# A fused attention and MLP kernel: pair sums for the middle heads of the second batch, and three block pairs begun before the attention ends

## The chip, the cores and the metric

The kernel runs on one core of a Trainium2 chip. The metric is the device time of one execution in microseconds (us), smaller is better. TensorE does the matmuls, VectorE and ScalarE the elementwise work, GpSimd a part of it, and SyncE (SP) issues most transfers.

## The reference

Eight batches, twelve heads, 448 positions, head size 64; then an MLP over the 3584 tokens.

```python
q_n, k_n = rmsnorm(q, g_q), rmsnorm(k, g_k)        # over the head's 64 numbers
scores = matmul(q_n, k_n.T) / sqrt(64)
attn = exp(scores - max); attn /= attn.sum(-1)
x = matmul(attn, v)                                # [3584, 768]: tokens x (heads * 64)
h = x @ w_in                                       # d_ff = 2048
out = gelu_tanh(h) @ w_out
```

All inputs and the output are float32; the kernel's matmuls take bf16.

## The kernel before

**Tiling.** One attention is one batch: three groups of four heads (c = 0, 1, 2; the "middle heads" are c = 1), seven tiles of 64 positions each. A *unit* (c, t) is the scores of one tile for four heads (`unit`, L335: four matmuls of 64x448 into one PSUM tile of two banks) and its exp (`exp`, L343, on ScalarE). So a batch has 21 units, 0 to 20; units 7 to 13 are the middle heads'. From the second attention on TensorE works in quarters of 64x64, four matmuls side by side.

**Behind the units.** "s" is the sum over the exps, a product with ones; "x" is the product with V (both `products`, L387). For some groups VectorE adds exps before "s" so that fewer matmuls are needed: `added(b, c)` says how many tiles are merged into one, and `add_exps` has the steps A (tiles 0,1 plus 2,3: two pair sums, L355), B (plus 4,5, L358), F (the two into one, L360), G (plus tile 6, L362). In batch 1 the first group adds seven tiles, the last six, and the middle group none: its "s" reads the seven exps, 28 matmuls. After "s" VectorE transposes the sums (T, `turned`, L397), takes reciprocals (R, `recip`, L402), spreads them (S, `spread`, L409) and multiplies "x" with them (M, `quad_x`, L422) into `xT`, which the MLP reads.

**Batch pipeline.** The attention of batch b+1 runs on TensorE mixed with the second MLP layer of the batch before (`quartered`, L495). After it comes the first layer of the batch (`mm1_turn`, L537), two 128-column blocks of w_in ("a pair") in one PSUM tile, in two turns, with a gelu per pair (L543). The last heads' `xT` comes late, so a pair can begin with the chunks of the first eight heads (`early`, four of six chunks) and take the last two (`late`) afterwards. `attention` begins pairs 0 and 1 that way at its end.

**What sets the order.** Every engine's order is written out by hand. `SECOND` (L577) is the second attention's: its first string mixes second-layer steps ("3r" is three steps of four matmuls) with units, "s" and "x"; its second string is the order of VectorE, where small letters and K, L are hooks for other work (`extra`): L0 and L1 load batch 2's q and k, K0 applies the gain to the DMA-transposed k of batch 1's last heads (`gain`, L325) and lets GpSimd go on to the squares for batch 2 (`gpsimd_waits`, L795, then L164), a0 to a5 reduce these squares (L173). VectorE's queue is in order: an entry that waits holds all behind it.

**PSUM.** Four tiles are handed out in turn by `pair`; the second layer holds one while it accumulates, so units, "s" and "x" take turns in three. `rsqrt_last` also takes one as scratch space.

**Transfers.** SP issues q and k loads, the stores and the DMA transposes (`dma_trans`, L319), in program order. `late_loads` and `late_transposed` first write one element of the destination on VectorE, so that SP issues the transfer only when VectorE has come to that place in its queue. GpSimd issues w_in, w_out and v on a queue of its own; the last part of w_out is wanted in the second attention.

**First attention.** `first_attention` (batch 0) runs the units with lists of side work per slot (`side`, `mid`); slot n of `mid` comes behind unit n and its exp.

Of the kernel before, what the change touches and what calls it, by code (L numbers as in the profile page):

```python
# [17 lines left out]
def kernel(  # L18
# [11 lines left out]
    nc = tc.nc  # L30
# [9 lines left out]
    NT = S // R  # L40
    NCH = H // 4
    HP = H // 2
# [95 lines left out]
    def late_loads(b, c):  # L138

        for n in "qk":  # L140
            for go in load(b, c, n):
                nc.vector.memset(raws[n, b, c][:1, 0, 0, :1], 0.0)
                go()
# [167 lines left out]
    def trans(b, c, eng=nc.vector):  # L311
        for n in "qk":
            turn(b, c, n)
            put(b, c, n, eng=eng)
# [12 lines left out]
    exs, ess, oas, scs = {}, {}, {}, {}  # L327
# [18 lines left out]

    def added(b, c):

        return NT - 1 if b > 1 else (NT - 1, 0, NT - 2)[c] if b else 0

    def add_exps(b, c, step):
        ex = exs[b, c]
# [18 lines left out]
    def products(b, c, what, lo=0, hi=NT):  # L371

        if lo == 0 and steady():
            o = oas["o", c, what] = pair("o")
            oas[what] = oas[c, what] = [o[:, r, :S] for r in range(2)]
        elif lo == 0:
            oas[what] = spare.pop() if spare else [o[:, :S] for o in oall]
        o = oas[what]
        es = [exs[b, c][:, t] for t in range(NT)]
        if not what and added(b, c):  # L380
            es[:added(b, c) + 1] = [ess[b, c][:, 0]]
        n = len(es)
        for i in range(lo, min(hi, n)):
            for r in range(2):
                rs = slice(r * R, (r + 1) * R)
                for a in range(2):
                    nc.tensor.matmul(  # L387
                        o[r][a * D:(a + 1) * D],
                        vb[b % 2][rs, 2 * c + a, i] if what else ones[rs], es[i][rs, a],
                        start=(i == 0), stop=(i == n - 1),  # L390
                    )
# [156 lines left out]
    def mm1_pair(i, cs=range(HP), b=0, js=range(2)):  # L548
# [19 lines left out]
    early, late = range(HP - 2), range(HP - 2, HP)  # L568
# [8 lines left out]
    SECOND = (  # L577
        "3r u 5r uu 8r u 8r uu 8r u 5r u 4r u 7r us 4r u 4r u 3r uu 4r x 1r usu 3r u 6r u 2r u 5r"
        " uu 10r x 6r sx",
        "A0 L0 B0 F0 G0 L1 T0 R0 K0 S0 a0 M0 a1 T1 a2 R1 a3 S1 A2 a4 B2 a5 F2 M1 T2 R2 S2 M2",  # L580
        {6: 0, 14: 1, 21: 2},
    )

    def attention(b, side, extra, ends):

        order, dve, evictions = STEADY if b > 1 else SECOND
        at = 0 if b % 2 else 3
        if b > 1:
            m, lo = HD // 2, b % 2 * HD
            tiles = [[(i, 0, HD), (i, HD, d_model)] for i in range(at, at + 3)]  # L590
            tiles.append([(6, lo, lo + m), (6, lo + m, lo + HD)])
        else:
            tiles = [[(0, 0, HD), (1, 0, HD)], [(2, 0, HD), (0, HD, d_model)],
                     [(1, HD, d_model), (2, HD, d_model)]]
        full, made = {}, {("unit", -1)}

        def second_layer():
            for k, parts in enumerate(tiles):
                def finished(o, k=k):
                    full[k] = o  # L600
                    made.add(("full", k))
                yield from quartered(parts, finished, late=b == 1 and k == 0)

        m2 = second_layer()
        units = [(c, t) for c in range(NCH) for t in range(NT)]
        scalar = []
        for n in range(len(units) + 1):
            if n in evictions:
                scalar.append(("E", evictions[n]))
            if n < len(units):  # L610
                scalar.append(("u", n))
        vector = [(w[0], int(w[1:] or 0)) for w in dve.split()]

        def needs(w, c):
            n = c * NT
            return {
                "u": [("unit", c)] + [("x", 0), ("T", 0)] * (c >= 2 * NT), "E": [("full", c)],
                "A": [("u", n + t) for t in range(4)], "B": [("u", n + 4), ("u", n + 5)],
                "G": [("u", n + 6)], "T": [("s", c)], "M": [("x", c)] + [("p", 1)] * (c == NCH - 1),
            }.get(w, [])  # L620

        def run(w, c, eng):
            if w == "u":
                exp(b, *units[c])
            elif w == "E":
                evict(b - 1 - (c == 3 and b % 2), tiles[c], full[c], eng)
            elif w in "ABFG":
                add_exps(b, c, w)
            elif w == "T":
                turned(c)  # L630
            elif w == "R":
                recip()
            elif w == "S":
                spread()
            elif w == "M":
                quad_x(b, c)
            else:
                for fn in extra.get(w + str(c), ()):
                    fn()
            made.add((w, c))  # L640

        def go_on():
            for queue, eng in ((vector, nc.vector), (scalar, nc.scalar), (vector, nc.vector)):
                while queue and made.issuperset(needs(*queue[0])):
                    run(*queue.pop(0), eng)

        n = {"u": 0, "s": 0, "x": 0}
        for fn in extra.get("first", ()):
            fn()
        for word in order.split():  # L650
            if word.endswith("r"):
                for _ in range(int(word[:-1])):
                    next(m2)
                    go_on()
                continue
            for w in word:
                k = n[w]
                n[w] += 1
                if w == "u":
                    for fn in side.get(k, ()):  # L660
                        fn()
                    unit(b, *units[k])
                    made.add(("unit", k))
                else:
                    last = added(b, k)
                    assert {("u", t) for t in range(k * NT, (k + 1) * NT)} <= made
                    assert w == "x" or not last or ("FG"[last - NT + 2], k) in made
                    products(b, k, "sx".index(w))
                    made.add((w, k))
                go_on()  # L670
        assert next(m2, None) is None and not scalar and vector == [("M", NCH - 1)]
        for fn in ends:
            fn()
        nc.scalar.preload_act_table_set(GELU_SET)
        if b == 1:
            for m in "qk":
                square(2, NCH - 1, m, nc.scalar)
        mm1_turn(b, 0, 0, early, begin=True)
        mm1_turn(b, 1, 0, early, begin=True)
        mm1_turn(b, 0, 1, early)  # L680
        mm1_turn(b, 1, 1, early)
        made.add(("p", 1))
        go_on()

# [172 lines left out]
    def turn_new(c, ts):  # L857
# [37 lines left out]
           (17, lambda: products(0, 1, 1, 3), lambda: quad_x(0, 1),  # L895
            lambda: total(1, 0, "q")),
           (18, lambda: spared(), lambda: products(0, 2, 0, 0, 3)),
           (20, lambda: products(0, 2, 0, 3, 5), lambda: products(0, 2, 1, 0, 5),
            lambda: products(0, 2, 0, 5, 6))]
    first_attention(plan(*side), plan(*mid))  # L900

# [4 lines left out]
    def late_transposed(b, c):  # L906

        for n in "qk":
            dst = kT if n == "k" else qT_of(b)
            nc.vector.memset(dst[:1, c, 0, 0, :1], 0.0)  # L910
        transposed(b, c)
# [8 lines left out]
    for b in range(B):  # L920
        m1, side, extra, ends = [], [], [], []
        if b == 0:
# [5 lines left out]
                  (2, lambda: total(1, 1, "q"), lambda: total(1, 1, "k"),  # L928
                   lambda: normed(1, 0, "q", nc.vector), lambda: rsqrt_last(1),
                   lambda: normed_both(1, 1, nc.vector)),  # L930
                  (6, lambda: trans(1, 0, nc.scalar), lambda: late_transposed(1, 2)),
                  (7, lambda: trans(1, 1))]
            extra += [("L0", lambda: late_loads(2, 0)), ("L1", lambda: late_loads(2, 1)),
                      ("a1", lambda: late_loads(2, 2)),
                      ("K0", lambda: gain(1, 2))]

            for n in "qk":
# [38 lines left out]
        for f in range(nf // 2 if b == 0 else nf):  # L976
            i, part = f // 4 * 2, f % 4
            if b == 0:
                if f == 2:
                    mm1(0, 5)  # L980
                    square(1, 1, "k", nc.scalar)
                elif f > 2:
                    mm1_pair(f)
            elif f == 1:
                mm1_turn(b, 0, 1, late)
                mm1_turn(b, 1, 1, late)
                mm1_turn(b, 0, 0, late, end=True)
            elif f == 3:
                mm1_turn(b, 1, 0, late, end=True)
            elif part == 1:  # L990
                mm1_turn(b, i, 0, range(HP), begin=True)
                mm1_turn(b, i + 1, 0, range(HP), begin=True)
                mm1_turn(b, i, 1, range(HP), end=True)
            elif part == 3:
                mm1_turn(b, i + 1, 1, range(HP), end=True)
            for fn in m1.get(f, ()):
                fn()
# [47 lines left out]
```

## Time and profile before

| what | us |
|---|---|
| median of 3 runs | 390.71 |
| the runs | 393.07, 390.71, 390.48 |
| the profiled execution's own time | 391.54 |
| its span, first to last instruction | 389.6 |
| TensorE busy | 380.9 |
| ScalarE busy | 278.7 |
| VectorE busy | 236.1 |
| GpSimd busy | 125.3 |

The span is one profiled execution; its own time is some 2 us more than the span, as launch and end lie outside. A row of a timeline has the start in us from the span's start, the length, the engine, the line and operation, what it writes and reads, and in brackets the idle time of the engine before it and what ended it. In the chain of work that ended last, a matmul's piece runs from the end of the piece before to its own end. "Time to landing" of a transfer is from its issue to the last byte's semaphore.

### The profile page before, as it was taken

How to read it: one execution, taken by the hardware profiler on the slowest of the kernel's cores; microseconds unless marked ns; L12 is line 12 of the kernel's file. 1: busy time of each engine (PE TensorE's matmuls, PEld its weight loads, DVE VectorE, ACT ScalarE, POOL GpSimd, SP SyncE). 2: the span in 40 equal slices, each digit the busy share in tenths (PEclk: the TensorE clock that was granted, in tenths of full speed). 3: DMA queues.
4: the chain of work that ended last, by engine and by line, in shares of the span. 5: the costliest groups of instructions: out<-in, count | busy, mean ns of one | idle time of the engine just before them, and what ended most of it. 6: DMA issues, size and time to landing. Idle time of an engine off the chain costs nothing.

```text
span 389.6 us, 17545 instructions
## 1 busy us (share of the span) xinstructions
PE 380.9 (98%) x8060; PEld 294.2 (76%) x8060; DVE 236.1 (61%) x367; ACT 278.7 (72%) x353; POOL 125.3 (32%) x108
## 2 busy tenths in 40 slices
PE   7899999999999999999999999999999999999996
PEld 5565577777888788877888788877888778887664
DVE  5998837975697259835589256953598204980010
ACT  6995499767994689757996589946897449944300
POOL 5986505384005540083102740064400900000000
PEclk9999999999999999999999999999999999999999
DMA  8999997999714992369822995159622721120033
GB/s 258 326 231 210 210 163 247 266 229 236 152 44 94 248 208 60 84 133 234 171 69 64 203 235 106 44 102 268 98 76 54 123 45 42 44 65 4 2 82 81
DMA packets 64446, 54.68 MB, mean 140 GB/s; under 512 B 37620, under 2 KB 60020, under 8 KB 64372
## 3 DMA queue, kind: packets, MB, share of 16 engines
q1 hardware_dynamic: 53936, 41.33, 44.0%
q0 software_dynamic: 10128, 11.80, 18.4%
q8 instruction: 63, 1.03, 1.1%
q10 hardware_dynamic: 308, 0.43, 0.3%
q14 instruction: 11, 0.09, 0.1%
HBM read 45.61 MB, written 11.01 MB: 145 GB/s over the span
## 4 chain that ended last, share of the span: by engine, by line
PE 92%; ACT 4%; DMA 1%; POOL 1%; SPq 0%; issue 0%; DVE 0%; DVEq 0%
PE t L537 33%; PE t L495 32%; PE t L387 9%; PE t L335 7%; PE t L463 5%; PE t L556 4%; ACT ex L343 4%; DMA rawq<-in_q_dram 1%; POOL g L164 1%; PE h L436 1%; PE tp L296 0%; PE o L387 0%; SPq L745 0%; SPq L124 0%; PE os L387 0%
## 5 line engine op out<-in xcount | busy, mean ns | idle before, releaser
L343 ACT ACTIVATE ex<-t,shift 128x896 bf16<-128x896 f32 x168 | 156.2, 1014 | 2.5 <-PE t L335 2.2
L495 PE MATMUL t<-wout,g 64*64 64x384 bf16 (+1 forms) x3456 | 151.2, 305 | 0.7 <-issue 0.7
L495 PEld LDWEIGHTS <-g 64*64 64x64 bf16 x3456 | 113.3, 107 | 20.3 <-issue 1.1
L537 PE MATMUL t<-xT,win 64*64 64x448 bf16 x2688 | 128.6, 349 | 0.0
L537 PEld LDWEIGHTS <-win 64*64 64x64 bf16 x2688 | 96.6, 107 | 30.6
L543 ACT ACTIVATE g<-t 128x896 bf16<-128x896 f32 x56 | 50.5, 915 | 57.2 <-PE t L537 57.2
L173 DVE TENSOR_REDUCE ss<-sq 128x14 f32<-128x896 f32 (+3 forms) x45 | 44.6, 996 | 53.5 <-ACT sq L162 48.9
L335 PE MATMUL t<-qT,kT 64*64 64x448 bf16 x672 | 58.7, 351 | 1.8 <-ACT ex L343 0.8
L355 DVE TENSOR_TENSOR es<-ex 128x1792 bf16<-128x1792 bf16 x20 | 21.2, 1058 | 32.2 <-ACT ex L343 32.2
L278 POOL TENSOR_TENSOR nrmq<-rawq,rinv 128x896 bf16<-128x896 f32 (+1 forms) x21 | 34.8, 1659 | 15.6 <-ACT rinv L205 12.0
L795 POOL COPY mark<-es 1x1 bf16<-1x1 bf16 x6 | 1.1, 176 | 117.2 <-DVE es L362 112.6
L278 POOL TENSOR_TENSOR nrmk<-rawk,rinv 128x896 bf16<-128x896 f32 x20 | 33.6, 1680 | 0.0
L387 PE MATMUL t<-ex,vb 64*64 64x448 bf16 x588 | 32.1, 350 | 0.0
L335 PEld LDWEIGHTS <-kT 64*64 64x64 bf16 x672 | 25.5, 106 | 7.6 <-DVE kT L305 1.6
L397 DVE STREAM_TRANSPOSE st<-t 128x448 f32<-128x448 f32 x42 | 24.7, 626 | 9.1 <-PE t L387 9.1
L387 PEld LDWEIGHTS <-vb 64*64 64x64 bf16 x672 | 23.6, 107 | 7.0 <-issue 0.8
L409 DVE STREAM_TRANSPOSE rb<-rc 128x896 f32<-128x896 f32 (+1 forms) x25 | 26.7, 1067 | 0.3
L422 DVE TENSOR_TENSOR xT<-t,rb 128x896 bf16<-128x896 f32 x21 | 22.8, 1086 | 1.4 <-ACT ex L343 0.7
L701 DVE COPY osb<-t 128x384 f32<-128x384 f32 (+1 forms) x4 | 2.0, 508 | 35.2 <-PE t L463 35.2
L513 ACT COPY osb<-t 128x768 f32<-128x768 f32 (+1 forms) x18 | 12.6, 701 | 14.0 <-PE t L495 14.0
L164 POOL TENSOR_TENSOR sq<-rawq 128x896 f32<-128x896 f32 (+1 forms) x9 | 13.6, 1514 | 27.4 <-DVE ss L173 27.4
L358 DVE TENSOR_TENSOR es<-es,ex 128x1792 bf16<-128x1792 bf16 x20 | 21.3, 1063 | 0.7 <-ACT ex L343 0.7
(103 smaller groups left out, 314.3 us busy)
## 6 DMA issues: line engine op xcount, KB each, us to landing
rawq<-in_q_dram SPq DMA_DIRECT2D x22, 448.0 KB, 4.7
rawk<-in_k_dram SPq DMA_DIRECT2D x22, 448.0 KB, 5.5
out_dram<-osb SPq DMA_DIRECT2D x42, 192.0 KB, 2.7
vb<-in_v_dram POOLq DMA_DIRECT2D x6, 672.0 KB, 6.8
win<-in_moe_w_in_dram POOLq DMA_DIRECT2D x8, 384.0 KB, 12.4
wout<-in_moe_w_out_dram POOLq DMA_DIRECT2D x3, 768.0 KB, 17.9
out_dram<-osb SPq DMA_DIRECT2D x24, 96.0 KB, 4.0
vb<-in_v_dram POOLq DMA_DIRECT2D x2, 448.0 KB, 15.8
```

What stands on the lines that cost most here:

```text
L173: nc.vector.reduce_sum(sss[b][:, seat(b, c), "qk".index(n), hs, ts], squares(b, c, n, hs, ts), axis=AX.X)
L278: eng.tensor_mul(nrms[n, b, c][:, ts].rearrange("p t a d -> p a t d"), raws[n, b, c][:, :, ts], root[:, :, ts].to_broadcast([P, 2, m, D]),)
L335: nc.tensor.matmul(sc[r * R:(r + 1) * R, a, :S], kT[rs, c, t, r], qT[b][rs, c, :, r], start=True, stop=True,)
L343: nc.scalar.activation(exs[b, c][:, t], scs.pop((b, c, t))[:, :, :S], AF.Exp, scale=scale, bias=shift)
L358: nc.vector.tensor_add(es, es, ex[:, 4:6])
L387: nc.tensor.matmul(o[r][a * D:(a + 1) * D], vb[b % 2][rs, 2 * c + a, i] if what else ones[rs], es[i][rs, a], start=(i == 0), stop=(i == n ...
L397: nc.vector.transpose(st[:, r].rearrange("p a b -> p (a b)"), o[r])
L409: nc.vector.transpose(oas["rb"][:, rs].rearrange("p r s -> p (r s)"), rc.to_broadcast([128, (rs.stop - rs.start) * m, 32]),)
L422: nc.vector.tensor_mul(xT[b][:, 2 * c:2 * c + 2], oas["o", c, 1][:, :, :S], oas["rb"])
L495: mm = nc.tensor.matmul(o[a * R:(a + 1) * R, bank, :hi - lo], g[rs, f, at:at + R], wout[rs, f, lo:hi], start=(n == 0), stop=(n == len(step ...
L537: mm = nc.tensor.matmul(h[a * R:(a + 1) * R, j, :S], win[rs, c, at:at + R], xT[b][rs, c], start=begin and c == cs[0], stop=end and c == cs ...
L543: nc.scalar.activation(g[:, 2 * i:2 * i + 2, (b % 2) * S:(b % 2 + 1) * S], h[:, :, :S], AF.Gelu_apprx_tanh,)
```

## The change

1. `added(1, 1)` becomes 3: VectorE does step A for the middle heads of batch 1 (a new entry A1 behind R0 in VectorE's order), and their "s" reads two pair sums and the last three exps, five tiles instead of seven.
2. At the end of batch 1's attention a third pair (2) begins with the first eight heads' chunks, both turns; later, at f = 5, pair 2 gets its last chunks, ends, and pair 3 begins.
3. In the first attention one step of the last heads' sums moves from slot 20 to slot 19.
4. The two DMA transposes for batch 1's last heads move from f = 6 of batch 0's first layer to L0, behind the first A0; the loads of batch 2's first heads move from L0 to the start of the attention. On SP the loads now stand ahead of the transposes, and the first stores and the next loads behind them.

```diff
     def added(b, c):
-        return NT - 1 if b > 1 else (NT - 1, 0, NT - 2)[c] if b else 0
+        return NT - 1 if b > 1 else (NT - 1, 3, NT - 2)[c] if b else 0
...
         if not what and added(b, c):
-            es[:added(b, c) + 1] = [ess[b, c][:, 0]]
+            es[:added(b, c) + 1] = [ess[b, c][:, i] for i in range(1 + (added(b, c) == 3))]
...
-        "A0 L0 B0 F0 G0 L1 T0 R0 K0 S0 a0 M0 a1 T1 a2 R1 a3 S1 A2 a4 B2 a5 F2 M1 T2 R2 S2 M2",
+        "A0 L0 B0 F0 G0 L1 T0 R0 A1 K0 S0 a0 M0 a1 T1 a2 R1 a3 S1 A2 a4 B2 a5 F2 M1 T2 R2 S2 M2",
...
         mm1_turn(b, 0, 1, early)
         mm1_turn(b, 1, 1, early)
+        if b == 1:
+            mm1_turn(b, 2, 0, early, begin=True)
+            mm1_turn(b, 2, 1, early)
...
-           (20, lambda: products(0, 2, 0, 3, 5), lambda: products(0, 2, 1, 0, 5),
+           (19, lambda: products(0, 2, 0, 3, 4)),
+           (20, lambda: products(0, 2, 0, 4, 5), lambda: products(0, 2, 1, 0, 5),
...
-                  (6, lambda: trans(1, 0, nc.scalar), lambda: late_transposed(1, 2)),
+                  (6, lambda: trans(1, 0, nc.scalar)),
...
-            extra += [("L0", lambda: late_loads(2, 0)), ("L1", lambda: late_loads(2, 1)),
-                      ("a1", lambda: late_loads(2, 2)),
+            extra += [("first", lambda: late_loads(2, 0)), ("L0", lambda: late_transposed(1, 2)),
+                      ("L1", lambda: late_loads(2, 1)), ("a1", lambda: late_loads(2, 2)),
...
+            elif b == 1 and f == 5:
+                mm1_turn(b, 2, 1, late)
+                mm1_turn(b, 2, 0, late, end=True)
+                mm1_turn(b, 3, 0, range(HP), begin=True)
```

More of the change, by code (lines that the diff above doesn't have):

```diff
@@ L666, in attention @@
                     assert {("u", t) for t in range(k * NT, (k + 1) * NT)} <= made
-                    assert w == "x" or not last or ("FG"[last - NT + 2], k) in made
+                    assert w == "x" or not last or ({3: "A", 5: "F", 6: "G"}[last], k) in made
                     products(b, k, "sx".index(w))
```

## The prediction

> **What bounds the kernel now.** I read the page first (busy shares, the chain that ended last), then busy time by stage, then the chain piece by piece around the edits, and last VectorE, ScalarE, GpSimd and the DMA queues in order of time from 48 to 80 us, where the edits lie.
>
> ```profile
> span 389.6 us, 17545 instructions
> PE 92%; ACT 4%; DMA 1%; POOL 1%; SPq 0%; issue 0%; DVE 0%; DVEq 0%
> 28.00:50.00 22.00, 22.00 (x170) 12.24 (x160) 18.96 (x46) 12.02 (x15) 12.68 (x11) 1.00 1.14 210
> 50.00:76.80 26.80, 26.10 (x599) 19.66 (x601) 19.32 (x36) 24.03 (x32) 8.31 (x10) 1.00 1.02 221
> 95.00:121.90 26.90, 26.90 (x703) 22.83 (x696) 20.89 (x30) 24.14 (x29) 2.81 (x4) 1.00 0.51 118
> ```
>
> The columns of the stages are length, then busy time of PE, weight loads, VectorE, ScalarE and GpSimd, the granted clock, the DMA share and GB/s. TensorE ends the chain for 92% of the span, at clock 1.00, and from 28 us on it has no idle time to the third attention but for 0.70 us, in the second attention (50.00 to 76.80). So matmul time that is taken away there is worth its full length, and so is every new stall: nothing later gives it back. The third attention on is not edited and moves as a block.
>
> The second attention, piece by piece, in the chain (start, length, what):
>
> ```profile
> 60.75 0.70 issue
> 65.83 0.19 PE t L335 x4
> 66.02 1.32 PE t L387 x28
> 67.35 0.19 PE t L335 x4
> 69.19 0.28 PE t L335 x4
> 76.80 18.22 PE t L537 x384
> ```
>
> After the 0.70 us hole come unit 14 (65.83), the sums of the middle heads (66.02), unit 15 (67.35) and unit 17 (69.19, 0.28 instead of 0.19: it waited a little).
>
> **What the change takes away.** The middle heads' sums go from 28 matmuls to 20: two of the pairs stand for four exps. From the row at 66.02, 8/28 of 1.32 us is **0.38 us**. In the first attention one step of four sum matmuls (1.32/7 = **0.19 us**) goes ahead of the last unit's scores, where TensorE idles 0.52 us:
>
> ```profile
> 27.62 0.38 PE L335 MATMUL t<-qT,kT 64*64 64x448 bf16 x4 [0.52 <-ACT ex L343]
> ```
>
> What follows is back to back until 60.75, so everything up to there comes 0.19 us sooner.
>
> **What it adds on VectorE.** The pair addition A1 stands after the reciprocal R0 and ahead of K0 (gain), S0 (spread), a total, M0 (xT of heads 0-3). In order of time before:
>
> ```profile
> 55.32 1.09 DVE L355 TENSOR_TENSOR es<-ex 128x1792 bf16<-128x1792 bf16 x1 [4.35 <-ACT ex L343]
> 61.45 0.33 DVE L402 RECIPROCAL rc<-st 128x28 f32<-128x28 f32 x1
> 61.69 0.35 DVE L325 TENSOR_SCALAR kT<-kT,gcols 128x896 bf16<-128x896 bf16 x1
> 61.96 1.11 DVE L409 STREAM_TRANSPOSE rb<-rc 128x896 f32<-128x896 f32 x1
> 64.00 1.09 DVE L173 TENSOR_REDUCE ss<-sq 128x14 f32<-128x896 f32 x1 [0.94 <-POOL sq L164]
> 65.78 1.09 DVE L422 TENSOR_TENSOR xT<-t,rb 128x896 bf16<-128x896 f32 x1 [0.69 <-ACT ex L343]
> 66.80 1.07 DVE L173 TENSOR_REDUCE ss<-sq 128x14 f32<-128x896 f32 x1
> 68.39 0.64 DVE L397 STREAM_TRANSPOSE st<-t 128x448 f32<-128x448 f32 x1
> 62.11 0.18 POOL L795 COPY mark<-kT 1x1 bf16<-1x1 bf16 x1 [17.52 <-DVE kT L325]
> L343 ACT ACTIVATE ex<-t,shift 128x896 bf16<-128x896 f32 x168 | 156.2, 1014 | 2.5 <-PE t L335 2.2
> 60.35 1.09 ACT L343 ACTIVATE ex<-t,shift 128x896 bf16<-128x896 f32 x1
> 62.04 1.91 ACT L343 ACTIVATE ex<-t,shift 128x896 bf16<-128x896 f32 x2 [0.60 <-PE t L335]
> 67.11 0.42 PE L335 MATMUL t<-qT,kT 64*64 64x448 bf16 x4
> ```
>
> A1 costs 1.09 us by the first row, but its wait costs more. It needs the exps of units 7 to 10, and unit 10's began at 62.04, after the reciprocal was done (61.78); so VectorE stands still, and with it all that is queued. K0 releases GpSimd's mark, which releases its squares, which the total ahead of M0 waits for: from the start of K0 to that total 2.31 us (61.69 to 64.00), then 1.02 us to the earliest start of M0 (66.80 to the next start at 67.82, the same operation).
>
> Who waits for M0: four PSUM tiles take turns and the second layer holds one, so unit 14, the sums and unit 15 use the other three, and unit 15 writes the tile that M0 reads. Before, M0 ended at 66.87 and unit 15 began at 67.11: 0.24 us to spare.
>
> The earliest end of it: exps follow each other by 0.89 us (1.91 for two, less one of 1.014, the mean of the page's group), so unit 10's exp could begin at 60.35 + 0.89 - 0.19 = 61.05 if the hole at 60.75 is gone. It ends at 62.06; A1 runs from 62.10, K0 from 63.13, the total from 65.44, M0 from 66.46 instead of 65.78: **0.68 us late**. The next chain behind M0 is dense on VectorE (total, the transposes of the sums until 69.03), and unit 17 waits for those transposes; from there on VectorE and TensorE were back to back to 76.8. So 0.68 us is carried to the end, and the 0.38 us of saved matmuls vanish in the wait. If the hole stays, unit 10's exp begins at 62.04 - 0.19 = 61.85 and M0 is **1.48 us late**. The trace names no engine as the hole's cause, so I cannot tell; I take the middle, **1.08**.
>
> **What is moved on the DMA queue.** The two loads of batch 2 leave when VectorE is done with batch 1's transposes (about 51.1) instead of at 56.46, and the two DMA transposes leave behind the first A0 (56.4) instead of at 48.43. The stores and the next loads, behind them on SP, come some 2 to 4 us later.
>
> ```profile
> 48.43 1.32 SPq L319 DMA_TRANSPOSE qT<-nrmq  x1
> 49.85 4.29 SPq L319 DMA_TRANSPOSE kT<-nrmk  x1
> 56.46 0.37 SPq L124 DMA_DIRECT2D rawq<-in_q_dram  x1
> qT<-nrmq SPq DMA_TRANSPOSE x1, 10.3
> kT<-nrmk SPq DMA_TRANSPOSE x1, 2.9
> kT<-nrmk SPq DMA_TRANSPOSE x1, 6.2
> ```
>
> The last three rows are times to landing: under the weights' stream, and of two later transposes. From 56.4 and one issue of 1.3 us, kT lands between 60.6 and 63.9, and K0 wants it at 63.13 to 64: hidden by A1's own wait, or late by at most 0.8. I take 0. GpSimd's second pair of squares would want its loads at about 67.5; issued 2 to 4 us after 60.56 they land at 67.5 to 69.5, and the totals that read them come 1.6 us behind: hidden.
>
> The loads now share the engines with the last part of w_out:
>
> ```profile
> L785 POOL DMA_DIRECT2D wout<-in_moe_w_out_dram x1: 723/723/723, 33.7 to 33.7; - x1
> wout<-in_moe_w_out_dram POOLq DMA_DIRECT2D x1, 384.0 KB, 20.5
> 53.58 1.30 PE t L495 x32
> q0 software_dynamic: 354, 0.39, 115.8%
> q0 software_dynamic: 362, 0.32, 97.7%
> q1 hardware_dynamic: 271, 0.07, 25.6%
> rawq<-in_q_dram SPq DMA_DIRECT2D x1, 448.0 KB, 5.7
> q1 hardware_dynamic: 106, 0.19, 104.3%
> ```
>
> It lands at 33.7 + 20.5 = 54.2. TensorE uses it from the seventh of eight steps of the row at 53.58, in the timeline 54.4: 0.2 us to spare, and TensorE comes 0.19 sooner. The queue rows are 50 to 52 us (alone, 0.39 MB) and 52 to 54 (0.32 MB beside the transposes). The last row is 60.5 to 61 us, loads alone: 0.38 MB/us. If the two loads (448 KB each, 0.9 MB) press the weights no more than the transposes did, the stall is 0; if they go wholly first, 0.9/0.38 = 2.4 us. I take **0.35**, near the low end, as 52 to 54 shows both queues moving, the weights at 82% of their speed. It falls ahead of the exps and shifts the whole chain to M0.
>
> The Trainium skill ("DMA: Bandwidth & Descriptors", queues, rings and completion order) says that a DMA engine goes round its queues packet by packet. That speaks against issuing the loads here, and the row with both queues moving agrees; with packets of like size it would halve the stream from about 52.2 us, and by it the stall would come out at some 0.6, an estimate, instead of my 0.35.
>
> **The three pairs begun early.** By 18.22/384 us a matmul, 64 early matmuls last 3.03 us, to 79.83; the last xT ended at 79.64:
>
> ```profile
> 78.55 1.09 DVE L422 TENSOR_TENSOR xT<-t,rb 128x896 bf16<-128x896 f32 x1
> ```
>
> No stall was there to be removed. With both engines equally late the cover of 0.19 us stays, and the third pair (96 matmuls, 4.54 us) makes it 1.7: insurance, worth 0. Pair 3 then wants pair 0's tile some 0.1 us before its gelu ends: 0 to 0.1, taken as 0.
>
> **The sum:** 1.08 + 0.35 = +1.4 us. The profiled execution took 391.54 us, which makes 393.0; that lay 0.83 above the median of the runs, 390.71, so the median should be **392.1**. With 0.68 + 0 to 1.48 + 0.8 (the weights at a third of their upper bound; beyond that it is a rival's case) the forecast's own range is 391.4 to 393.0.
>
> **The rivals.**
> *No wait at unit 15 (faster).* If M0 comes in time, only savings are left: 0.38 + 0.19, and 0.70 more if the hole closes: 389.4 to 390.1. It decides if M0 ends before 66.5. For it: the trace of before shows no wait of a matmul for xT. Against it: M0 would have to end 1.0 us sooner than the earliest chain allows (66.46 + 1.09). Chance 0.15.
>
> *kT lands late (slower).* Had the transposes their 10.3 us again from 56.4, kT would be there at 67 to 68; unit 14 and M0 wait for K0, M0 ends about 4.4 us after K0's start, near 72 instead of 66.87: +5, 395.7. It decides from 63.9 on, microsecond for microsecond. For it: the loads are in front of them on the same queue. Against: the 6.2 us above are of a transpose that stood behind two such loads as well. Chance 0.10.
>
> *The weights stall TensorE (slower).* At 2.4 us the sum is 1.08 + 2.4 = 3.5, 394.2. Against: both queues moved together in 52 to 54. Chance 0.10.
>
> **How the numbers follow.** The forecast has 0.65. The range 390.2 to 394.2 takes in the weights rival and leaves out most of the fast one and the late kT. A measurement of this kernel tells about 1% (3.9 us) from no change. Faster by over 1% needs 386.8, beyond every case: 0.01. Slower by over 1% is 394.6: most of the late kT and a tail of the weights, 0.08. Within 1%: 0.91.
>
> **What would show it.** Right: in the changed kernel VectorE idles about 0.5 to 1.6 us before the middle heads' es; M0 starts at 66.4 to 67.6; unit 15 shows an idle gap on TensorE put down to xT; the sums have 20 matmuls; the move from the second attention's end on is constant at +0.7 to +2.3. Wrong: unit 15 follows the sums at once (the tile rotation or the chain over GpSimd is misread), or K0 waits for a DMA, or a hole at 54.2 longer than 1 us.

## The result and the profile after

| | before | after |
|---|---|---|
| median, us (6 runs each) | 390.77 | 393.63 |
| lowest to highest, us | 390.48 to 393.07 | 393.50 to 393.94 |
| profiled execution's own time, us | 391.54 | 393.62 |
| its span, us | 389.6 | 391.8 |

The changed kernel is slower by 2.86 us; the ratio is 1.0064, 95% interval 1.0048 to 1.0080. That lies inside the stated range of 390.2 to 394.2 and inside 1%, but above the forecast's own 391.4 to 393.0, and it is twice as far from before as forecast. One run of the kernel before, in the rounds of experiments 1, 3, 4 and 6, took 1032.31 us and is left out of their ratios.

The page of the changed kernel (the span, the chain by engine, and the group of the first layer's weight loads) and its second attention, with the columns of the prediction's stage rows:

```profile
span 391.8 us, 17531 instructions
PE 87%; ACT 5%; DMA 2%; issue 2%; POOL 1%; DVE 1%; SPq 1%; DVEq 0%; POOLq 0%; ACTq 0%
L537 PEld LDWEIGHTS <-win 64*64 64x64 bf16 x2688 | 94.2, 107 | 33.7 <-PE t L537 1.5
50.23:77.74 27.51, 25.73 (x586) 18.94 (x588) 20.18 (x39) 23.72 (x32) 8.03 (x9) 1.00 0.88 208
```

TensorE's share of the chain falls from 92% to 87%; what comes in is issue (0 to 2%) and one per cent each of DMA, ScalarE, VectorE and SP. The second attention (the last row) now holds 1.78 us in which TensorE does nothing. The first layer's weight loads, whose idle time had no releaser before, now waited 1.5 us for matmuls.

The second attention on TensorE (timeline, from the middle heads' sums on; ahead of them TensorE has no idle time any more):

```profile
65.27 0.57 PE L387 MATMUL t<-es,ones 64*64 64x448 bf16 x8
65.65 0.76 PE L387 MATMUL t<-ex,ones 64*64 64x448 bf16 x12
68.06 0.38 PE L335 MATMUL t<-qT,kT 64*64 64x448 bf16 x4 [1.65 <-DVE rawk L142]
68.92 1.17 PE L495 MATMUL t<-wout,g 64*64 64x384 bf16 x24
70.23 0.38 PE L335 MATMUL t<-qT,kT 64*64 64x448 bf16 x4
```

The sums have 8 + 12 = 20 matmuls, and unit 15 waits 1.65 us. The named releaser is a tiny memset that VectorE issues right behind xT; what unit 15 waits for is that xT. Unit 17 (70.23) waits too: 24 matmuls of the second layer last 0.98 us by the rows of 0.81 for 20 in the chain, so it could have begun at 69.90 and is 0.33 us late.

VectorE in the same stretch:

```profile
62.56 1.09 DVE L355 TENSOR_TENSOR es<-ex 128x1792 bf16<-128x1792 bf16 x1 [0.59 <-ACT ex L343]
63.57 0.45 DVE L325 TENSOR_SCALAR kT<-kT,gcols 128x896 bf16<-128x896 bf16 x1
...
65.92 1.09 DVE L173 TENSOR_REDUCE ss<-sq 128x14 f32<-128x896 f32 x1 [0.89 <-POOL sq L164]
66.93 1.08 DVE L422 TENSOR_TENSOR xT<-t,rb 128x896 bf16<-128x896 f32 x1
69.53 0.64 DVE L397 STREAM_TRANSPOSE st<-t 128x448 f32<-128x448 f32 x1
```

VectorE idles 0.59 us for unit 10's exp, A1 (62.56) holds the gain K0 (63.57 instead of 61.69), the total waits for GpSimd's squares, and xT of heads 0 to 3 starts at 66.93 instead of 65.78. The transpose of the sums, 68.39 before, starts at 69.53, and unit 17 follows it.

The chain in the first layer of batch 1:

```profile
77.94 3.81 PE t L537 x80
81.75 0.04 issue
81.79 2.87 PE t L537 x56
84.66 0.04 issue
84.71 1.74 PE t L537 x32
86.44 0.04 issue
86.49 10.41 PE t L537 x216
```

Before it was one piece, 18.22 us for 384 matmuls; now it is broken three times and ends 96.90 - 77.94 = 18.96 us after its start.

To follow the experiments I cut each trace at the first matmul of each stage, TensorE's starts on both sides (us). "Rest" is the profiled execution's own time less the four stages ahead.

| kernel | second attention starts | second attention | first layer, batch 1 | third attention | rest | own time |
|---|---|---|---|---|---|---|
| before | 50.03 | 26.57 | 18.22 | 26.84 | 269.88 | 391.54 |
| after | 50.23 | 27.51 | 18.98 | 27.03 | 269.87 | 393.62 |
| difference | +0.20 | +0.94 | +0.76 | +0.19 | 0.0 | +2.08 |

In the row of before the second attention includes the hole. From its start to the middle heads' sums it took 15.76 us before and 15.04 after, so the hole was worth 0.72; without it the row would be 25.85, and the change makes that 1.66 longer. The start of the second attention lay between 49.8 and 51.3 us in the profiles shown here, and this scatter blurs the medians. In all but two of them it was there before batch 0's first layer began (30.0 to 31.1 us); in experiments 4 and 10 TensorE waited in that layer as well, 0.5 and 0.8 us for the DMA of w_in.

### The profile page after: what moved, and what is told of

The parts are those of the page before. It is cut to its first block, busy times and chain, and to the rows that moved or that the text cites. A ratio compares the mean times of both kernels' runs of the same rounds, so it can differ in the third digit from the quotient of the medians.

```text
span 391.8 us, 17531 instructions
## 1 busy us (share of the span) xinstructions
PE 382.4 (98%) x8052; PEld 290.0 (74%) x8052; DVE 237.1 (61%) x368; ACT 278.6 (71%) x353; POOL 125.2 (32%) x108
## 4 chain that ended last, share of the span: by engine, by line
PE 87%; ACT 5%; DMA 2%; issue 2%; POOL 1%; DVE 1%; SPq 1%; DVEq 0%; POOLq 0%; ACTq 0%
PE t L537 33%; PE t L495 29%; PE t L387 8%; PE t L335 7%; PE t L463 5%; ACT ex L343 5%; PE t L556 4%; DMA rawq<-in_q_dram 1%; POOL g L164 1%; DMA kT<-nrmk 1%; PE h L436 1%; SPq L319 0%; DVE st L397 0%; PE o L387 0%; POOL sq L164 0%
## 5 line engine op out<-in xcount | busy, mean ns | idle before, releaser
L495 PEld LDWEIGHTS <-g 64*64 64x64 bf16 x3456 | 111.6, 107 | 20.5
L537 PEld LDWEIGHTS <-win 64*64 64x64 bf16 x2688 | 94.2, 107 | 33.7 <-PE t L537 1.5
L355 DVE TENSOR_TENSOR es<-ex 128x1792 bf16<-128x1792 bf16 x21 | 22.2, 1059 | 32.8 <-ACT ex L343 32.8
```

The source lines that it names most:

```text
L355: nc.vector.tensor_add(es, ex[:, :2], ex[:, 2:4])
L495: mm = nc.tensor.matmul(o[a * R:(a + 1) * R, bank, :hi - lo], g[rs, f, at:at + R], wout[rs, f, lo:hi], start=(n == 0), stop=(n == len(step ...
L537: mm = nc.tensor.matmul(h[a * R:(a + 1) * R, j, :S], win[rs, c, at:at + R], xT[b][rs, c], start=begin and c == cs[0], stop=end and c == cs ...
```

## The experiments

Each is the changed kernel with one edit, unless said otherwise, timed in rounds beside the kernel before on the same chip.

**1. The addition behind K0 and S0 (add_later).**

```diff
-... R0 A1 K0 S0 a0 M0 ...
+... R0 K0 S0 A1 a0 M0 ...
```

> The changed kernel with A1 moved behind K0 and S0 in VectorE's order, nothing else. Theory (place): unit 15 waits because A1's wait for unit 10's exp holds K0, K0 holds GpSimd's squares, and these hold the total ahead of M0. With K0 first, M0 should start near 65.4 instead of 66.9, the 1.65 us idle before unit 15 should shrink to 0.3 at most, and the time should fall by 1.3 to 1.6 us, to 392.0 to 392.3. Rival (load): VectorE simply has 1.1 us too much to do there; the addition still stands ahead of M0, so M0 comes no earlier than 66.5 and the time stays at 393.2 or more.

Measured: 392.98 us, ratio 1.0049 (1.0037 to 1.0061), 0.65 below the changed kernel; second attention 26.57 instead of 27.51. VectorE's timeline, then GpSimd's:

```profile
61.69 0.35 DVE L325 TENSOR_SCALAR kT<-kT,gcols 128x896 bf16<-128x896 bf16 x1
62.98 1.88 DVE L355 TENSOR_TENSOR es<-ex 128x1792 bf16<-128x1792 bf16 x1
65.78 1.07 DVE L422 TENSOR_TENSOR xT<-t,rb 128x896 bf16<-128x896 f32 x1
...
62.24 1.67 POOL L164 TENSOR_TENSOR sq<-rawq 128x896 f32<-128x896 f32 x1
63.88 2.52 POOL L164 TENSOR_TENSOR sq<-rawk 128x896 f32<-128x896 f32 x1
```

K0 and xT start at 61.69 and 65.78, the very times of before. So it was the place of A1, ahead of K0, that made xT late. Unit 15's wait falls from 1.6 to 0.7 us (waits of TensorE). It doesn't vanish, since the sums are 0.38 us shorter and the hole no longer holds TensorE back: unit 15 comes sooner than before and wants a tile that is free no sooner.

A1 took 1.88 us here instead of 1.09. It began at 62.98, while the first squares ran until 63.91, and ended 0.95 us behind them; the second squares, begun at 63.88, took 2.52 instead of 1.67 us. Each lost about 0.8 us, nearly the time that the other had left (0.93) or still needed (0.95): they took turns. The Trainium skill ("SBUF — State Buffer", who interferes with whom) states that a VectorE instruction with two SBUF inputs and a GpSimd instruction that reads SBUF exclude each other, the later one blocking until the first is done; these rows agree.

**2. The squares behind the addition (squares_later).** As 1, and GpSimd's mark and squares wait for A1 instead of K0, so that the two can't overlap.

```diff
-... R0 A1 K0 S0 a0 M0 ...
+... R0 K0 S0 A1 X0 a0 M0 ...
-extra.append(("K0", lambda: gpsimd_waits(kT[:1, 2, 0, 0, :1])))
+extra.append(("X0", lambda: gpsimd_waits(ess[1, 1][:1, 0, 0, :1])))
-("K0", ... square(2, c, n, nc.gpsimd, hs)),
+("X0", ... square(2, c, n, nc.gpsimd, hs)),
```

> The kernel with A1 behind K0 and S0, in which A1 took 1.88 us instead of 1.09, with one thing changed: GpSimd's squares wait for A1's result instead of for K0's, so they run behind A1 and not beside it. Theory (the two engines get in each other's way): A1 takes 1.05 to 1.1 us. Rival (it is slow because of where it stands, behind a transpose): 1.8 to 1.9 again. As the squares now come later, M0 is late again and the time is near 393.4; the length of A1 is what is asked.

Measured: 394.75 us in one run, second attention 27.73 (another 0.65 us came in the seventh attention, see 5). VectorE:

```profile
63.46 1.05 DVE L355 TENSOR_TENSOR es<-ex 128x1792 bf16<-128x1792 bf16 x1
66.41 1.09 DVE L173 TENSOR_REDUCE ss<-sq 128x14 f32<-128x896 f32 x1 [1.90 <-POOL sq L164]
67.41 1.08 DVE L422 TENSOR_TENSOR xT<-t,rb 128x896 bf16<-128x896 f32 x1
```

The addition takes 1.05 us again: the 0.8 us in 1 come from GpSimd's squares running beside it. And the late squares make the total and xT late again (1.90 us of waiting), which is the chain that the prediction named.

**3. xT ahead of the total (xt_first).**

```diff
-... A1 K0 S0 a0 M0 a1 ...
+... A1 K0 S0 M0 a0 a1 ...
```

> The changed kernel with M0 ahead of the total a0 in VectorE's order, A1 left where it is. Theory (chain over GpSimd): M0 no longer waits for the squares and starts near 65.05, when the spread is done, so unit 15 comes without a wait near 66.4; but both totals and the transposes of the sums now stand behind it, the second total waits for GpSimd until 67.5, the transposes end near 69.7, and unit 17 waits in unit 15's place until about 69.8 instead of 70.2: 0.4 us gained, 393.2. Rival (M0 is late because of A1's own length): unit 15 still waits over 1 us.

Measured: 393.65 us, ratio 1.0070 (1.0057 to 1.0083), as the changed kernel; second attention 27.14, 0.37 less. In the profiled run (394.27) a second attention that began 0.73 later took this back; why the median isn't lower, no run here shows. Waits of TensorE between 50 and 80 us, and VectorE:

```profile
PE t L335 <- DVE st L397: 1.5, 1, 1.5
65.90 1.09 DVE L422 TENSOR_TENSOR xT<-t,rb 128x896 bf16<-128x896 f32 x1
68.29 1.09 DVE L173 TENSOR_REDUCE ss<-sq 128x14 f32<-128x896 f32 x1 [0.30 <-POOL sq L164]
```

Unit 15 no longer waits, but unit 17 waits 1.5 us for the transposes behind the totals. Both waits have the same root, VectorE about 1 us behind; moving one entry only chooses which unit pays.

**4. No addition (no_add).** The middle heads' sums read seven exps again; all else as changed.

```diff
-        return NT - 1 if b > 1 else (NT - 1, 3, NT - 2)[c] if b else 0
+        return NT - 1 if b > 1 else (NT - 1, 0, NT - 2)[c] if b else 0
-... R0 A1 K0 S0 ...
+... R0 K0 S0 ...
```

> The changed kernel without the pair addition: the middle heads' sums read the seven exps again (28 matmuls) and A1 is gone; the third pair, the moved step and the moved transfers stay. Theory: the wait at unit 15 goes, the 0.38 us of matmuls come back, and what is left over the kernel before is the first layer's 0.74 us: 391.6 to 392.2. Rival (the transfers or the step cost something too): 392.6 or more. If the addition were a gain, the time would be above 393.6.

Measured: 391.80 us (8 runs), ratio 1.0025 (1.0013 to 1.0036), 1.83 below the changed kernel. Second attention 25.99, third 26.81, first layer 18.98. So the addition, net of the 0.38 us that it saves, costs 1.83 by the medians, 1.52 + 0.22 by the stages: two thirds of the loss. What is left over before, +0.9 by the medians, is about the first layer's 0.76.

**5. The third pair dropped (two_pairs).**

```diff
-        if b == 1:
-            mm1_turn(b, 2, 0, early, begin=True)
-            mm1_turn(b, 2, 1, early)
...
-            elif b == 1 and f == 5:
-                mm1_turn(b, 2, 1, late)
-                mm1_turn(b, 2, 0, late, end=True)
-                mm1_turn(b, 3, 0, range(HP), begin=True)
```

> The changed kernel without the third early pair: the first layer of batch 1 is begun and taken up as in the kernel before; the addition, the moved step and the moved transfers stay. Theory (drain): the first layer goes back from 18.98 to 18.2 or 18.3 us, and the time falls by 0.7 us to 392.9; the last xT (80.78 in the changed kernel's profile) meets the end of the 64 early matmuls (80.77) within 0.1 us, so the third pair covers nothing. Rival (the third pair is needed): TensorE waits for the last xT and the time stays at 393.4 or more.

Measured: 393.53 us, ratio 1.0053 (1.0033 to 1.0074) against a before of 391.12 on that chip. The chain:

```profile
77.96 18.22 PE t L537 x384
```

One piece of 18.22 again, and no wait for the last xT: two pairs are cover enough although VectorE is later, and the third is worth -0.76 us. The median shows little of it (0.1 us; 0.4 by the ratios). In the profiled run 0.39 us came back in the seventh attention, 27.23 instead of 26.84, far behind the edit. The same stage took 0.34 more in experiments 6 and 9 and 0.65 more in 2. In 2 the chain has there

```profile
286.09 0.61 PE t L495 x13
286.70 0.34 issue
```

a break inside a row of second-layer matmuls that nothing in the trace releases, like the hole of before (11). In 5, 6 and 9 the chain breaks behind the same 13 matmuls, for 0.08 us or less.

**6. The turns kept apart (turns_apart).** All three pairs, but no two turns of one pair in succession.

```diff
+        if b == 1:
+            mm1_turn(b, 2, 0, early, begin=True)
         mm1_turn(b, 0, 1, early)
         mm1_turn(b, 1, 1, early)
         if b == 1:
-            mm1_turn(b, 2, 0, early, begin=True)
             mm1_turn(b, 2, 1, early)
...
                 mm1_turn(b, 2, 1, late)
-                mm1_turn(b, 2, 0, late, end=True)
                 mm1_turn(b, 3, 0, range(HP), begin=True)
+                mm1_turn(b, 2, 0, late, end=True)
```

> The changed kernel with the turns of the early pairs interleaved: pair 2 begins ahead of the second turns of pairs 0 and 1, and pair 3 begins between pair 2's two last parts, so that no two turns of one pair stand back to back. Theory (drain): each of the three back-to-back changes of turn costs about 0.25 us, because the second turn waits for the first one's last matmul to finish and nothing else is queued between; they go, the first layer is 18.2 us instead of 18.96, and the time falls by 0.6 to 0.75 us to 392.9 to 393.0. Rival (the extra 0.74 us has another cause, such as pair 3 waiting for pair 0's gelu or late xT): no change, 393.5 or more.

Measured: 393.38 us, ratio 1.0063 (1.0050 to 1.0075); first layer 18.61. The chain:

```profile
77.53 5.70 PE t L537 x120
...
83.25 0.93 ACT g L543
...
84.22 11.92 PE t L537 x248
```

The three breaks are gone, so they were the turn changes: 18.98 - 18.22 = 0.76, or 0.25 us each. When a pair's turn changes, its next matmul waits for the last one of the turn before (`follows` in `mm1_turn`); with another pair's turn between them that wait is over unseen, with nothing between, TensorE stands still. The Trainium skill ("TensorE: Matmul & The Clock Gate", single matmul latency) gives, for one matmul over the full array, a constant of about 166 ns on top of the time of its columns. These matmuls are quarters; 0.25 us with the weight load behind the wait is of that size, and no run here splits it. One new break took their place: pair 3, begun earlier, waits for the gelu that frees pair 0's tile, about 0.4 us (18.61 - 18.22).

**7. The transfers as before (old_transfers).**

```diff
-                  (6, lambda: trans(1, 0, nc.scalar)),
+                  (6, lambda: trans(1, 0, nc.scalar), lambda: late_transposed(1, 2)),
...
-            extra += [("first", lambda: late_loads(2, 0)), ("L0", lambda: late_transposed(1, 2)),
-                      ("L1", lambda: late_loads(2, 1)), ("a1", lambda: late_loads(2, 2)),
+            extra += [("L0", lambda: late_loads(2, 0)), ("L1", lambda: late_loads(2, 1)),
+                      ("a1", lambda: late_loads(2, 2)),
```

> The changed kernel with the transfers where they stood before: the two DMA transposes leave at f = 6 of the layer before, batch 2's first loads at L0. Theory (the hole belongs to this order): the hole of some 0.8 us on TensorE near 60.75 comes back, unit 10's exp and with it the whole chain to M0 is later by that much, and the time is 394.2 to 394.5. Rival (the hole was one execution's accident): no hole and 393.6. The addition and unit 15's wait stay in both.

Measured: 393.81 us, ratio 1.0064 (1.0045 to 1.0082); second attention 27.52, the same to 0.01, and no hole at 60.75. The move of the transfers neither costs nor brings anything here, and the hole is gone without it too.

**8. A new order (reordered).** The third pair dropped, A1 behind K0, xT ahead of the total, and the later totals spread.

```diff
-"... R0 A1 K0 S0 a0 M0 a1 T1 a2 R1 a3 S1 A2 a4 B2 a5 F2 M1 ..."
+"... R0 K0 S0 A1 M0 a0 T1 a1 R1 a2 a3 S1 A2 a4 a5 B2 F2 M1 ..."
```

> The changed kernel with two early pairs as before, and VectorE's order T0 R0 K0 S0 A1 M0 a0 T1 a1 R1 a2 a3 S1 A2 a4 a5 B2 F2 M1 T2 R2 S2 M2: nothing that waits for GpSimd stands ahead of M0, and the transposes of the sums stand ahead of the second total. Theory: M0 starts by 65.0, unit 15 and unit 17 wait 0.2 us together at most, the second attention is 25.4 to 25.9 us long (25.7 before without its hole, 27.5 in the changed kernel), the first layer 18.2 to 18.4, and the time is 390.4 to 391.0: the change's loss is undone and the 0.38 us of matmuls just show or are just spent. Rival (VectorE has too much to do at all): the wait moves to unit 17 or to the last sums, and the time stays above 391.5.

Measured: 392.18 us (12 runs), ratio 1.0028 (1.0011 to 1.0046); nine runs from 391.8 to 392.5 and three from 393.7 to 394.0. The profiled one is of the three:

```profile
63.90 0.45 DVE L325 TENSOR_SCALAR kT<-kT,gcols 128x896 bf16<-128x896 bf16 x1 [1.93 <-DMA kT<-nrmk]
...
77.35 0.38 PE L387 MATMUL t<-es,ones 64*64 64x448 bf16 x4 [0.96 <-DVE es L360]
```

K0, which now wants kT at 61.97, waits 1.93 us for the transpose, and the middle heads' sums on TensorE wait 1.9 us in their turn for A1 behind it. That is the prediction's rival of the late kT. The transpose of k took 4.69 us to land here and 2.91 in the changed kernel, where it was there at 61.67, 1.9 us before K0 behind A1 asked for it. Of the nine faster runs there is no profile, so that only the three have this wait is not shown. The last row is the wait of the last heads' sums, which experiment 9 has too.

**9. The new order with the old transfers (old_reordered).** The edits of 7 and 8, and the ones written by two memsets instead of three (see 10).

> The reordered kernel (two early pairs, VectorE's order T0 R0 K0 S0 A1 M0 a0 T1 a1 R1 a2 a3 S1 A2 a4 a5 B2 F2 M1 T2 R2 S2 M2) with the transfers where they stood in the kernel before, and with the ones written by two memsets instead of three. In the reordered kernel's profile K0, which now comes first, waited 1.93 us for the DMA transpose of k, and its runs fell in two groups near 391.9 and 393.9. Theory (transposes that leave 8 us earlier are there when K0 wants them): K0 does not wait, no run near 393.9, the second attention is 25.5 to 26.0 us long and the time 390.5 to 391.1, equal to the kernel before within its noise. Rival (the hole near 60.75 comes with the early transposes): 0.8 us more on TensorE, 391.3 to 391.9.

Measured: 391.91 us (12 runs), ratio 1.0021 (1.0009 to 1.0032) against a before of 391.15. VectorE, then TensorE:

```profile
61.84 0.35 DVE L325 TENSOR_SCALAR kT<-kT,gcols 128x896 bf16<-128x896 bf16 x1
63.14 1.88 DVE L355 TENSOR_TENSOR es<-ex 128x1792 bf16<-128x1792 bf16 x1
...
61.51 0.35 PE L495 MATMUL t<-wout,g 64*64 64x384 bf16 x3 [0.61 <-issue]
76.09 0.38 PE L387 MATMUL t<-es,ones 64*64 64x448 bf16 x4 [0.96 <-DVE es L360]
```

K0 is in time, and none of the units waits. The hole is there again, 0.61 us; with it and 0.34 us more in the seventh attention the profiled run, 393.02, is the slowest of the twelve. The time of A1 now comes out at the end: the last heads' sums wait 0.96 us for the addition F2. No order that I tried beats the kernel before: VectorE is busy for 14.12 of the 15 us between 61 and 76, and 1.1 to 1.9 us of additions there buy 0.38 us of matmuls.

**10. One instruction less on VectorE (one_less).** The changed kernel with the ones written by two memsets at the very start.

```diff
-    for i in range(3):
-        nc.vector.memset(ones[:, i * D // 4:(i + 1 + i // 2) * D // 4], 1.0)
+    for i in range(2):
+        nc.vector.memset(ones[:, i * D // 2:(i + 1) * D // 2], 1.0)
```

> The changed kernel with the ones written by two memsets instead of three, so that VectorE's stream again has as many instructions ahead of the third attention as before. In every profile with A1 the transposes of the sums of the third attention start about 0.37 us late and that attention is 27.03 us long instead of 26.84; without A1 it is 26.81. Theory (place in the instruction stream: one instruction more pushes a border of the stream onto a place where TensorE waits): 26.84 again. Rival (A1 itself does it, by the turn of the es buffers): 27.03 still.

Measured: 394.43 us in one run that began its second attention 0.95 later. In the changed kernel's third attention a transpose on VectorE starts late and holds a unit (chain):

```profile
107.97 0.27 issue
108.24 1.19 DVE st L397 x2
```

With one instruction less this break is gone and the third attention takes 26.81 instead of 27.03, as with the addition left out (26.81). So the 0.2 us do not belong to what A1 does. The expectation's "every profile with A1" overlooks experiment 8, which has A1 and three memsets and took 26.84. Counted in the traces, the transpose is 0.35 us late in each of the seven profiles with 191 VectorE records ahead of it, waits included, and in time in the six with 189 or 190, experiment 8 among them. The delay goes with that number; why, no run here shows.

**11. The kernel before once more (before_again).**

> The kernel before, unchanged, profiled once more. The question is the hole of 0.8 us on TensorE near 60.75. Theory (it comes now and then): the second attention is 25.7 us long and the span near 388.8, as the median of the runs (390.8) against the profiled 391.5 suggests. Rival (it belongs to this kernel): 26.57 again.

Measured: 391.61 us in one run, second attention 26.22. The chain:

```profile
60.53 0.64 PE t L495 x13
61.17 0.35 issue
```

The hole is there again, behind the same 13 matmuls, at half its length. It is in both profiles of before and in old_reordered, and not in the changed kernel or with the old transfers put back (7). It comes and goes with edits elsewhere and always stands behind the same matmul, the 733rd of the trace. No run here tests what makes it; it stays open.

## Why the prediction was right, and where it was not

The sign, the 1% and the mechanism of the main term held: A1 waits for unit 10's exp, holds K0, the squares and xT, and unit 15 waits for the PSUM tile. Its steps in turn:

- **Late xT.** Forecast: start at 66.46 to 67.26, measured 66.93; VectorE idle 0.5 to 1.6, measured 0.59; none of the signs named as wrong came. Of those named as right one failed: the move is not constant from the second attention's end on, but 1.14 us there, 1.90 behind the first layer and 2.09 behind the third attention. Experiments 1 and 2 show the link from K0 over the squares to xT.
- **What is carried to the end, 1.08.** Measured 0.94 against the profiled run of before. The parts: unit 15 begins 1.85 us behind its turn (65.27 and 20 matmuls of 0.047 make 66.21, it began at 68.06), unit 17 follows unit 15 by 2.17 instead of 1.97, 0.20 more, 0.38 is saved, 0.72 of the hole is gone: +0.95.
- **The hole, the middle of two cases.** It is gone in the changed kernel. Then M0 should have been 0.68 late by my sum; from 65.78 it was 1.15 late, 0.95 without the 0.20 by which all began later. The 0.27 between are there when A1 starts (62.56, forecast 62.10, less 0.20): unit 10's exp ended that much later than I had worked it out from two rows.
- **The weights, 0.35: nothing.** From 28.20 to 66.40 TensorE has no idle time, and the last part of w_out had landed by 32.5 + 20.4 = 52.9 us (windows, then the tile's groups):

```profile
28.20:66.40 38.20, 38.20 (x534) 23.42 (x526) 27.83 (x62) 28.19 (x35) 13.83 (x13) 1.00 1.03 206
L788 POOL DMA_DIRECT2D wout<-in_moe_w_out_dram x5: 703/752/812, 26.2 to 32.5; - x5
DMA to landing us min/median/max: 15.5/18.5/20.4
```

  GpSimd issued it 1.2 us sooner than in the profile of before (33.7), and the two loads, issued at 51.25 and 51.71, moved nothing before 53.5, so they never met the last part of w_out. A margin of 0.2 us read from one execution said little, and the rule by which I had 0.6 had no stall to decide. The 0.6 was also too small for its rows: at half of 0.39 MB in 2 us, the 0.32 MB of the second row take 3.3 us, a stall of about 1.3. With the old transfers (7) the stage was the same, which says that the loads' place costs nothing.
- **kT, nothing.** Right in the changed kernel, and in 1, where K0 came at 61.69 and did not wait; 8 shows how near it was: without A1 ahead of K0 it cost 1.93 us in the profiled run.
- **The third pair, "insurance, worth 0": the step that failed.** It costs 0.76 us, three changes of turn without another pair between them (5 and 6). I counted matmuls and PSUM tiles and not the wait in `mm1_turn` that makes the second turn follow the first. What I named as insurance covered nothing. The small term beside it, pair 3's wait for pair 0's gelu, is 0 here and 0.4 only when pair 3 begins earlier (6).
- **The first attention's moved step, -0.19: nothing.** The step runs in the idle time ahead of the last unit, but the stage isn't shorter. The chain before, then after:

```profile
27.62 0.38 PE t L335 x4
28.38 1.14 PE o L387 x20
30.27 0.86 PE t L556 x4
```

```profile
27.82 0.38 PE t L335 x4
28.39 0.18 PE o L387 x2
28.58 1.13 PE o L387 x18
30.47 3.13 PE t L556 x16
```

  From the last unit's scores to the MLP it is 2.65 us both times. The sums end 0.19 sooner, and the 20 products behind them take 0.17 longer (0.18 + 1.13 against 1.14); my "back to back until 60.75" did not hold there, and no run shows why.
- **The third attention, not foreseen:** +0.19; by experiment 10 it goes with the number of VectorE instructions ahead.
- **From the profiled run to the median.** The sum for the profiled execution was 393.0, measured 393.62. I then took off 0.83, since before's profiled run lay that far above its median. The changed kernel's profiled run lies at its median (393.62, 393.63) and its runs within 0.44 of each other, where those of before spread over 2.6. So of the miss of 1.5 us, 0.6 are terms and 0.8 are this step. The 0.6 is small by luck: 0.35 for the weights and 0.14 of the carried time were forecast too high, while 0.76, 0.19 and a start 0.20 later were not foreseen. It is luck too that the stated range held: the median lies above the forecast's own 393.0, and the range reached to 394.2 for the weights rival, which did not come. The hole, 0.70 and 0.35 in two profiles of before, and the start-up are what was seen to vary; that the fast runs of before have no hole was not seen.

Of the rivals, "no wait at unit 15" was wrong in the changed kernel (3 brings it about, and unit 17 waits instead), the weights did nothing, and the late kT did not come in the changed kernel, though it did in 8.

## What to carry to other kernels

An addition that saves matmuls pays only where its engine has slack at that place: here the wait ahead of it and the queue behind it cost about 1.8 us more than the 0.38 us saved, and moving it only moved the wait from unit 15 to unit 17 to the last sums. When work is begun early "for safety", look at how its pieces follow each other and not only at whether they fit: here each turn that depended on the one just before it cost 0.25 us. A margin of a few tenths of a us, or a profiled run above its median, read from one execution is scatter until a second one shows it.

## What the runs showed of the hardware

- VectorE's addition of two SBUF tiles took 1.05 to 1.09 us alone and 1.88 beside GpSimd's squares, which themselves went from 1.67 to 2.52: the two engines took turns (1, 9), and without the overlap the 1.05 was back (2).
- A TensorE turn that waited for the last matmul of the turn just before it cost about 0.25 us at a granted clock of 1.00 (5, 6).
- The third attention changed by 0.2 us with one tiny VectorE instruction more or less at the program's start (10), and the seventh by up to 0.65 between kernels that differ only far ahead of it (2, 5, 6, 9). In the second case, as in the hole of before, TensorE stands still behind 13 matmuls of a row, waiting for nothing that the profile shows.
